# Three slots for the tanh of r, and wider identity products at the start of a gated-recurrence and feed-forward kernel

## The chip, the core and the metric

The kernel runs on one core of one Trainium2 chip. The metric is the device time of an execution in microseconds (us). A profile of one execution lies beside it: its span is the time from the first to the last instruction, and the device time is a few us longer. Engines: PE is TensorE (PEld its weight loads), ACT ScalarE, DVE VectorE, POOL GpSimd, SP the queue that issues the DMAs.

## What is computed

```python
# x, r_gate, i_gate: 4 x 5824 x 256 fp32; a_param: 256
a_base = 1 / (1 + exp(-a_param))
log_a  = 8 * sigmoid(r_gate) * log(clip(a_base))
a_t    = exp(log_a)
norm   = sqrt(maximum(1 - a_t * a_t, 1e-6))
h[t]   = a_t[t] * h[t-1] + norm[t] * sigmoid(i_gate[t]) * x[t]      # scan along the sequence
y      = h.reshape(23296, 256)
out    = (((y @ w1) * (y @ w2)) @ w3) @ w_out                       # 256 -> 1024 -> 256
```

The last two weights are multiplied once at the start (w3 @ w_out, 1024 x 256), so that the main part has three products: y @ w1, y @ w2 and their elementwise product times the folded weight.

## The kernel before

The 23,296 tokens are cut into 47 chunks: two of 256, forty-four of 512, one of 256. A chunk goes through these steps, each a short word in one long string, ORDER, that is read from left to right at the end of the function; the word names the step, the number behind it the chunk. The string is written out by hand or by a planner, and each engine executes its instructions in just that order. Waits come from the tiles: an instruction waits until its inputs are written, and a new tile waits until those who used the slot before have done.

- r, i, x: loads of the three inputs into rings of 4, 5 and 4 slots, issued on SP (line 136).
- R: tanh of r / 2 on ScalarE, with tokens on the partitions, into a bf16 tile th_r (line 145 for the chunks in TURN_R, line 147 for the other 40).
- V: th_r is turned so that channels lie on the partitions. The seven chunks in TURN_R go through TensorE (a product with the identity in transpose mode, line 185, into PSUM), the other 40 through a DMA transpose that SP issues (line 196) into a tile rt.
- d: exp on ScalarE (line 207) gives a_t; s, q: its square and the root of 1 minus it (lines 215, 217, 221).
- I, p, t: tanh of i, plus 1, times x, into a tile u_t; U: u_t is turned as th_r is.
- g, h, y: the gated input, the scan on VectorE (line 249) and the cast to bf16 (line 258).
- a, b: products with w1 and w2 on TensorE (line 268) into PSUM tiles pa and pb; c: pa is copied to SBUF as sa (lines 282, 284); m: sa times pb on VectorE (line 296).
- D: product with the folded weight (line 307); e, o: copied out of PSUM and stored.
- Lw, Cw, Ft, Fc, Fm, Fe: loads, casts and the folding of the weights, all in the first 50 us or so.
- W0 to W15: sixteen heaps of products of the identity with itself, on TensorE (line 263). Nobody reads what they write. They stand in the first part of ORDER, at places where TensorE waits for its first data. The first is ahead of V1; six stand in a row ahead of the turns of U0; two between these turns and those of U1, four behind them, ahead of the first product with w1; three single ones follow later.

A helper, `ring(pool, shape, dtype, name, tag)`, gives the tiles: RINGS holds the number of slots of each tag, and a new tile takes the next slot in turn. th_r has two. So the tanh of a chunk waits for the turn of the chunk whose tanh was two before it in ORDER. The heaps take a tile of tag pb, which has two slots of two PSUM banks each, and which the products with w2 share.

Of the kernel before, what the change touches and what calls it, by code (L numbers as in the profile page):

```python
# [22 lines left out]
def kernel(  # L23
# [12 lines left out]
    nc = tc.nc  # L36
    P = 128
# [11 lines left out]
    CT = 512  # L49
# [16 lines left out]
    ident = consts.tile([P, P], BF16, tag="ident")  # L66
# [31 lines left out]
    STAGE = {'w1': ['a', 'a'], 'w2': ['nrm', 'nrm'], 'wo': ['a', 'nrm'], 'w3': ['a', 'nrm', 'a', 'nrm', 'a', 'nrm',  # L98
        'a', 'nrm']}
    CASTING = set()  # L100
    WARM = [8, 8, 8, 8, 8, 8, 8, 8, 8, 8, 8, 8, 8, 8, 8, 8]
    RINGS = {"r": 4, "i": 5, "x": 4, "th_r": 2, "u": 2, "rt": 2, "ut": 6, "a": 6, "nrm": 6, "h": 2, "y": 4,
             "sa": 3, "g": 3, "ot": 3, "w3": 4, "w3t": 2, "po": 4, "pb": 2}
    taken = dict.fromkeys(RINGS, 0)

    def ring(pool, shape, dtype, name, tag):
        slot = taken[tag] % RINGS[tag]
        taken[tag] += 1
        return pool.tile(shape, dtype, name=name, tag=f"{tag}_{slot}")
# [150 lines left out]
    def warm(i):  # L260
        pp = ring(psum_b, [P, 2, CT], F32, name="warm", tag="pb")
        for _ in range(WARM[i]):
            nc.tensor.matmul(out=pp[:, 0, :P], lhsT=ident, rhs=ident, start=True, stop=True)  # L263

    def up(c, m, dst, w_sb):
        w = sizes[c]
# [150 lines left out]
    def last(c):  # L417
# [15 lines left out]
        "Cwo.": partial(cast_w, "wo"), "Cw3.": partial(cast_w, "w3"),  # L433
        "Ft": fold_t, "Fc": fold_c, "Fm": fold_m, "Fe": fold_e,
        "W": warm, "E": cast_ident, "A3.": rates_turn, "A0.": rates_abs, "A1.": rates_exp, "A2.": rates,
    }

# [171 lines left out]
```

## Time and profile before

| what | value |
|---|---|
| time, median of 3 runs | 517.56 us (516.88 to 517.66) |
| span of the profiled execution | 513.8 us |
| TensorE clock granted | 1.000 |
| identity products | 128, 10.2 us busy, between 2.3 and 21.3 us |
| tanh of r, line 147 | 40, 1065 ns in the mean |
| tanh of r, line 145 | 7, the last at 85.6 us |
| DMA turns of th_r, from issue to landing | 2.4 / 4.4 / 7.1 us (min / median / max) |

In the lines of the profile below, a group is read as line, engine, operation, the tile written and those read, and the shape; "busy" is the union of its instructions' times. Chains of waits and timelines give start and length in us, and "x8" means eight instructions merged into one row. Waits give the total time, the number of times and the longest. A row of one line's own view gives the shortest, the median and the longest duration in ns.

### The profile page before, as it was taken

Reading aid. Unit: us, or ns where it says so; the run is one execution under the profiler, and the core shown is the slowest. Engines: PE = TensorE matmul, PEld = TensorE weight load, DVE = VectorE, ACT = ScalarE, POOL = GpSimd, SP = SyncE. Lnnn points to the kernel's source line nnn. Section 1 sums busy time; section 2 is a strip of 40 time slices with the busy share of each in tenths; the row PEclk is TensorE's granted clock in tenths of the full one; section 3 lists DMA queues with packets and bytes.
Section 4 is the critical chain, followed back from the end, with each engine's and each line's share of the span. In section 5 each row is a group of like instructions: output and inputs, shape, how many; then the busy total and the mean of one; then the engine's idle time right before and its main releaser. Section 6 shows DMA issues by size and latency. Waiting matters only on the chain.

```text
span 513.8 us, 9036 instructions
## 1 busy us (share of the span) xinstructions
PE 499.8 (97%) x3267; PEld 314.2 (61%) x3321; DVE 430.6 (84%) x414; ACT 465.5 (91%) x720; POOL 312.9 (61%) x271
## 2 busy tenths in 40 slices
PE   7889999999999999999999999999999999999997
PEld 7658565566565566556656556564566655656566
DVE  5889999999999889978878799888878697959762
ACT  8899999999999999999999999998998979888543
POOL 2583858646637956866595983957646569480200
PEclk9999999999999999999999999999999999999999
DMA  8997999999989998896999996989795995252112
GB/s 299 410 414 255 305 315 285 312 240 316 314 242 269 266 276 261 221 276 201 289 288 310 262 272 191 234 228 246 197 265 132 215 316 170 101 150 76 54 60 103
DMA packets 177281, 123.82 MB, mean 241 GB/s; under 512 B 86354, under 2 KB 172884, under 8 KB 177236
## 3 DMA queue, kind: packets, MB, share of 16 engines
q1 hardware_dynamic: 177232, 123.23, 84.6%
q8 instruction: 26, 0.43, 0.3%
q14 instruction: 19, 0.16, 0.1%
q10 hardware_dynamic: 4, 0.00, 0.0%
HBM read 78.91 MB, written 23.86 MB: 200 GB/s over the span
## 4 chain that ended last, share of the span: by engine, by line
PE 86%; ACT 5%; DMA 4%; issue 2%; DVE 2%; SPq 1%; ACTq 0%; DVEq 0%
PE po L307 29%; PE pb L268 28%; PE pa L268 27%; DMA r_t<-in_r_gate_dram 4%; ACT sa L284 2%; PE pw L378 1%; PE ptr L185 1%; DVE g_t L296 1%; PE ptw L367 1%; ACT ot L284 1%; SPq L136 1%; DVE h_t L249 1%; ACT i_t L154 1%; ACT a_t L207 1%; ACT L154 0%
## 5 line engine op out<-in xcount | busy, mean ns | idle before, releaser
L296 DVE TENSOR_TENSOR g_t<-sa,pb 128x1024 bf16<-128x1024 bf16 (+1 forms) x188 | 219.0, 1181 | 62.0 <-PE pb L268 29.1
L268 PEld LDWEIGHTS <-w_sb 128*128 128x128 bf16 x1504 | 146.3, 98 | 146.8 <-issue 5.5
L284 ACT CAST sa<-pa 128x512 bf16<-128x512 f32 (+1 forms) x339 | 182.4, 588 | 27.6 <-PE pa L268 18.3
L268 PE MATMUL pa<-y_t,w_sb 128*128 128x512 bf16 (+1 forms) x721 | 185.9, 372 | 4.5 <-ACT sa L284 3.5
L268 PE MATMUL pb<-y_t,w_sb 128*128 128x512 bf16 (+1 forms) x729 | 182.5, 372 | 1.5
L307 PE MATMUL po<-wp_sb,g_t 128*128 128x256 bf16 x1456 | 177.7, 273 | 0.4
L307 PEld LDWEIGHTS <-g_t 128*128 128x128 bf16 x1456 | 142.4, 98 | 40.5 <-issue 0.9
L258 POOL CAST y_t<-h_t 128x1024 bf16<-128x1024 f32 (+1 forms) x46 | 51.2, 1112 | 141.2 <-DVE h_t L249 138.8
L178 POOL TENSOR_TENSOR u_t<-i_t,x_t 128x512 bf16<-128x512 f32 (+1 forms) x89 | 120.0, 1365 | 5.5 <-DMA ut<-u_t 2.5
L249 DVE TENSOR_TENSOR_SCAN h_t<-a_t,h_t,nrm 128x512 f32<-128x512 f32 (+1 forms) x92 | 121.0, 1345 | 1.9
L217 POOL TENSOR_TENSOR nrm<-a_t 128x512 f32<-128x512 f32 (+1 forms) x74 | 81.3, 1116 | 12.8 <-ACT a_t L207 9.9
L207 ACT ACTIVATE a_t<-rt,la 128x512 f32<-128x512 bf16 (+1 forms) x80 | 64.2, 821 | 0.0
L159 POOL TENSOR_SCALAR i_t<-i_t 128x1024 f32<-128x1024 f32 (+1 forms) x45 | 53.4, 1189 | 17.6 <-ACT i_t L154 17.6
L284 ACT COPY ot<-po 128x512 f32<-128x512 f32 (+1 forms) x85 | 49.6, 590 | 11.8 <-PE po L307 11.5
L232 DVE SCALAR_TENSOR_TENSOR nrm<-nrm,ut 128x1024 f32<-128x1024 f32 (+1 forms) x39 | 54.4, 1394 | 5.2 <-ACT nrm L221 5.2
L154 ACT ACTIVATE i_t<-i_t 128x1024 f32<-128x1024 f32 (+1 forms) x47 | 49.2, 1049 | 0.1
L221 ACT ACTIVATE nrm<-nrm 128x1024 f32<-128x1024 f32 (+1 forms) x47 | 48.4, 1040 | 0.2
L147 ACT ACTIVATE th_r<-r_t 128x1024 bf16<-128x1024 f32 (+1 forms) x40 | 42.6, 1065 | 0.0
L282 DVE CAST sa<-pa 128x512 bf16<-128x512 f32 (+1 forms) x37 | 21.9, 617 | 1.4 <-PE pa L268 1.1
L221 ACT ACT_TABLE_LOAD x17 | 21.8, 1283 | 0.4
L215 ACT ACTIVATE nrm<-a_t 128x512 f32<-128x512 f32 (+1 forms) x17 | 10.7, 648 | 0.1
L263 PE MATMUL warm<-ident 128*128 128x128 bf16 x128 | 10.2, 247 | 0.0
(57 smaller groups left out, 132.6 us busy)
## 6 DMA issues: line engine op xcount, KB each, us to landing
out_dram<-ot SPq DMA_DIRECT2D x90, 256.0 KB, 3.4
r_t<-in_r_gate_dram SPq DMA_DIRECT2D x44, 512.0 KB, 5.3
i_t<-in_i_gate_dram SPq DMA_DIRECT2D x44, 512.0 KB, 5.9
x_t<-in_x_dram SPq DMA_DIRECT2D x44, 512.0 KB, 5.9
wf<-in_moe_w_dram SPq DMA_DIRECT2D x12, 512.0 KB, 10.1
wf<-in_moe_w_out_dram SPq DMA_DIRECT2D x2, 512.0 KB, 10.5
r_t<-in_r_gate_dram SPq DMA_DIRECT2D x3, 256.0 KB, 2.7
i_t<-in_i_gate_dram SPq DMA_DIRECT2D x3, 256.0 KB, 3.8
```

The lines of the kernel that those rows point to most:

```text
L154: nc.scalar.activation(out=t[:, :n, :], in_=t[:, :n, :], func=AF.Tanh, scale=0.5)
L159: (nc.vector if c in DV_PLUS else nc.gpsimd).tensor_scalar(t, t, 1.0, 1.0, op0=ALU.add, op1=ALU.mult)
L178: (nc.vector if (c, half) in DV_HALF else nc.gpsimd).tensor_mul(out=u, in0=t, in1=xt)
L207: nc.scalar.activation(out=a, in_=pr, func=AF.Exp, scale=la4[:, cb:cb + 1], bias=la4[:, cb:cb + 1])
L217: (nc.vector if (c, cb) in DV_SQUARE else nc.gpsimd).tensor_mul(out=n, in0=a, in1=a)
L221: nc.scalar.activation(out=T["n", c][:, :, :w], in_=T["n", c][:, :, :w], func=AF.Sqrt, scale=-1.0, bias=1.0)
L232: nc.vector.scalar_tensor_tensor(out=T["n", c][:, :, :w], in0=T["n", c][:, :, :w], scalar=1e-3, in1=T["pu", c][:, :, :w], op0=ALU.max, op1 ...
L249: nc.vector.tensor_tensor_scan(h[:, cb, :], a[:, cb, :], n[:, cb, :], init, ALU.mult, ALU.add)
L268: nc.tensor.matmul(out=dst[:, :w], lhsT=w_sb[:, cb, m * P:(m + 1) * P], rhs=T["y", c][:, cb, :w], start=(cb == 0), stop=(cb == NCB - 1))
L284: nc.scalar.copy(out=dst, in_=src_ps)
L296: nc.vector.tensor_mul(out=T["g", c][:, 2 * mp:2 * mp + 2, :w], in0=T["sa", c, mp][:, :, :w], in1=T["pb", c, mp][:, :, :w])
L307: nc.tensor.matmul(out=po, lhsT=T["g", c][:, k, j * P:(j + 1) * P], rhs=wp_sb[:, k, :], start=(k == 0), stop=(k == KD - 1), skip_group_che ...
```

## The change

Two tables and one instruction are changed. The ring of th_r gets a third slot: the tanh of a chunk now waits for the turn of the one three before it. SBUF tiles that are placed behind it move up by one slot, 2 KB a partition. Each of the sixteen heaps of identity products has two matmuls instead of eight. Each of them has the identity, repeated four times along the columns, as its moving operand, and writes 512 columns, a whole PSUM bank, where it wrote 128. ORDER is unchanged.

```diff
-    WARM = [8, 8, 8, 8, 8, 8, 8, 8, 8, 8, 8, 8, 8, 8, 8, 8]
-    RINGS = {"r": 4, "i": 5, "x": 4, "th_r": 2, "u": 2, "rt": 2, "ut": 6, "a": 6, "nrm": 6, "h": 2, "y": 4,
+    WARM = [2] * 16
+    RINGS = {"r": 4, "i": 5, "x": 4, "th_r": 3, "u": 2, "rt": 2, "ut": 6, "a": 6, "nrm": 6, "h": 2, "y": 4,
              "sa": 3, "g": 3, "ot": 3, "w3": 4, "w3t": 2, "po": 4, "pb": 2}
...
     def warm(i):
         pp = ring(psum_b, [P, 2, CT], F32, name="warm", tag="pb")
         for _ in range(WARM[i]):
-            nc.tensor.matmul(out=pp[:, 0, :P], lhsT=ident, rhs=ident, start=True, stop=True)
+            nc.tensor.matmul(out=pp[:, 0, :].rearrange("p (n q) -> p n q", q=P), lhsT=ident,
+                             rhs=ident.unsqueeze(1).broadcast_to([P, CT // P, P]), start=True, stop=True)
```

## The prediction

> **What bounds the kernel now.** I read the page first, then the chain of waits cut to its first 36 us, then ScalarE's waits, then the rows of the two tanh lines, and last the timeline of TensorE.
>
> The page's head and its chain:
>
> ```profile
> span 513.8 us, 9036 instructions
> ...
> PE 499.8 (97%) x3267; PEld 314.2 (61%) x3321; DVE 430.6 (84%) x414; ACT 465.5 (91%) x720; POOL 312.9 (61%) x271
> ...
> PE 86%; ACT 5%; DMA 4%; issue 2%; DVE 2%; SPq 1%; ACTq 0%; DVEq 0%
> ```
>
> TensorE is busy 97% of the span and carries 86% of the chain. Cut into stretches, busy time against length is 99.42 of 100 us between 200 and 300, 99.19 between 300 and 400, 99.42 between 400 and 500. Summed over 30 to 500 us TensorE is idle for 3.10 us. So from about 30 us on the time is the sum of the matmuls, and neither edit touches one of those.
>
> The start is different. This is the chain before 36 us (start, length, what):
>
> ```profile
> 5.24 8.59 DMA r_t<-in_r_gate_dram
> ...
> 13.91 10.40 DMA r_t<-in_r_gate_dram
> ...
> 24.37 1.28 ACT L145
> 25.67 1.06 ACT th_r L145
> 26.72 0.67 ACT a_t L207
> 27.39 0.27 ACT sa L284
> ...
> 27.70 0.38 PE pa L268 x2
> ```
>
> Two loads of r stand behind each other from 5.24 to 24.30 us, while the DMA engines run at 1.04 to 1.06 busy and 406 to 413 GB/s (10 to 25 us). ScalarE waits for the second one (r4), then TensorE waits for ScalarE. All the identity heaps lie before 21.3 us, in the shadow of this.
>
> **What the Trainium skill says.** "TensorE: Matmul & The Clock Gate", Part 1: start to start a matmul costs N/1.2 GHz while the clock is cold (106.7 ns for 128 columns, 426.7 for 512) and N/2.4 GHz plus about 2.5 ns when warm (55.6 and 215.7). The clock is lifted after a busy window of some 3.4 us whose phase is free; it counts time, not instructions. The trace agrees. The heap row below has 48 products in 4.38 us; less one latency (219 ns, the median of the row) that is 4.16 us for 47 steps, 88.5 ns each. With 107 and 56 ns that makes 30 cold ones, 3.2 us, so the lift is at about 8.7 us. Counted by half microseconds, the products are 7 or 8 up to 8.5 us and 13 from 9.0 on. "PSUM — Partial Sum Buffer", the four PSUM rules: one matmul writes at most one bank, 512 fp32 columns; the new product fills just that. "SBUF — State Buffer", Who interferes with whom: TensorE reads through its own ports and waits for no other engine. No run here tests that alone.
>
> **The identity products.** Sixteen heaps of 8 matmuls over 128 columns become sixteen heaps of 2 over 512: the same 1024 columns. The heaps in the timeline of TensorE:
>
> ```profile
> 2.31 1.03 PE L263 MATMUL warm<-ident 128*128 128x128 bf16 x8
> ...
> 5.48 4.38 PE L263 MATMUL warm<-ident 128*128 128x128 bf16 x48
> 9.70 0.39 PE L185 MATMUL ptr<-ident,u_t 128*128 128x128 bf16 x4
> 9.92 1.06 PE L263 MATMUL warm<-ident 128*128 128x128 bf16 x16
> 10.82 0.39 PE L185 MATMUL ptr<-ident,u_t 128*128 128x128 bf16 x4
> 11.04 1.95 PE L263 MATMUL warm<-ident 128*128 128x128 bf16 x32
> 12.97 1.03 PE L268 MATMUL pa<-y_t,w_sb 128*128 128x256 bf16 x8
> ```
>
> First heap: 8 x 107 = 856 ns becomes 2 x 427 = 854. In the run of six, the cold 3.2 us stays, and the 18 warm products, 18 x 56 = 1008 ns, become 4.5 x 216 = 972. The 72 products after 9.9 us (16, 32 and three heaps of 8) go from 72 x 56 = 4.03 us to 18 x 216 = 3.89. Together 0.18 us less of TensorE. The weight loads go from 128 to 32, 96 x 98 ns = 9.4 us of PEld, but they run beside the products (56 ns a step is the product's own rate), so nothing more. Since TensorE's array sees the same columns at the same rate, I expect the lift at the same place.
>
> What of the 0.18 us reaches the end? The heaps hold back the turns of u (ptr) and the first pa. The first four turns end at 9.70 + 0.39 = 10.09, and VectorE's product that reads them starts at 10.29 because of ScalarE's root, whose first of two ends about 9.63 + 1.15 / 2 = 10.21. So an earlier end of the heaps gives nothing there. The first pa (12.97) follows the cast of y_t, 12.30 + 0.61 = 12.91, and not the heap, which ended at 12.77 + its latency. The last two heaps (19.64, 20.66) are followed by 2.19 us of TensorE waiting for ScalarE at 27.70. The cover is the r4 load; were it gone, the most is the whole 0.18. I take 0, bounds -0.18 and, if a moving operand that repeats its 128 columns four times were read at half the rate (no row here has such an operand; the nearest, pa and po, read plain runs), twice the duration of the 24 matmuls ahead of the first pa: 24 x 216 ns = 5.2 us, less the slack worked out under the slower rival, so +3.9. Nothing in the trace or the pages gives a reason for that, so it gets the far edge only.
>
> The tile that a heap takes (tag pb) and its place in the ring don't change, so the waits before it and the next pb tile's stay.
>
> **The third slot.** ScalarE's tanh of r in chunk c wrote the slot of the tanh two before, so it waited for that chunk's turn: 7 chunks are turned by TensorE, 40 by DMA. With three slots it waits for the turn three before. ScalarE's waits (us in total, times, longest), and then two rows of line 147's own view (min/median/max ns, first and last start):
>
> ```profile
> ACT sa L284 <- PE pa L268: 18.3, 28, 2.5
> ACT ot L284 <- PE po L307: 11.5, 12, 3.3
> ACT sa L284 <- DVE g_t L296: 8.2, 9, 1.6
> ACT th_r L145 <- DMA r_t<-in_r_gate_dram: 1.6, 2, 0.9
> ```
>
> ```profile
> L147 ACT ACTIVATE th_r<-r_t x40: 645/1070/1143, 46.6 to 449.1; 128x1024 bf16<-128x1024 f32 x39, 128x512 bf16<-128x512 f32 x1
> L147 ACTq EVENT_SEMAPHORE  x8: 17/17/17, 48.1 to 338.7; - x8
> ```
>
> In the list of waits no tanh waits for a turn at all: its only waits are for r's own load, 1.6 us and 1.2 for its table load. The page's group of line 147 has 0.0 us of idle before its 40 tanhs. I then laid the start of each tanh beside the issue of the DMA turn two tanhs before: the closest pair is chunk 12's tanh at 85.64 with chunk 11's turn issued at 80.53, 5.11 us; the next is 6.48, all others 7.0 or more. The turn's landing takes 4.4 us at the median, 7.1 at most. So the wait was always over. The single one that might have bound, r4's tanh, needed chunk 3's turn by TensorE, whose products start at 23.30 and end at 23.91, before its load at 24.30. Gain of the slot: 0. Bounds: the 0.1 us idle before line 147's table loads, and the eight semaphore instructions there, 8 x 17 ns = 0.14, if they vanish. Nothing waits more, because the instruction order on each queue is unchanged and the added wait is older than the removed one.
>
> What else moves: the tiles behind th_r in SBUF lie 2 KB further on. 2,048 is a multiple of the 16-byte lines that the SBUF page names, so I cost it at 0.
>
> **The sum.** 513.8 - 0 to 0.3 = 513.5 to 513.8 of span. The median of the runs, 517.56, lies 3.76 above the span; so 517.5.
>
> **Rivals.** *Faster*: my reading of the waits is too coarse, and the looser slot lets a stretch like 178 to 197 us, where the chain leaves TensorE for ScalarE and VectorE, close up. For it: ScalarE is 91% busy. Against it: ScalarE works in a fixed order and no tanh waits. Price: TensorE's idle between 30 and 500 us is 3.10 us in all; half of it gone gives 516.0. *Slower*: the clock. If two long products a heap do not lift it as eight short ones do, all heaps run cold. Six heaps then last 12 x 427 = 5.12 us, 0.98 more; the 16 and the 32 products 0.85 and 1.71 more; eight turns 8 x 51 = 0.4. The first pa comes 3.9 us late. It decides from the point where the slack is used up: 0.12 us at the root (10.09 against 10.21) and the 1.18 us that ScalarE idles before r4 at 24.37, 1.3 together. What is over, 2.6 us, shifts all of TensorE's later work: 520.2. (All of this is an estimate from the rows above and the cold price.) Against it: the array is busy for the same time. *Scatter*: with three runs 0.78 us apart, the same work may land anywhere in 516.5 to 518.6.
>
> **How the numbers follow.** A difference within 0.2% (1.0 us) is about what a measurement of this kernel cannot tell from none. No change 0.68, faster 0.14, slower 0.18 (the cold clock 0.10, something in the 2 KB shift or the repeated operand 0.08). The likeliest case has 516.5 to 518.6; the range reaches to the faster rival's 516.0 and some way to 520.2, so 516.0 to 519.4.
>
> **What would show it.** After: 32 products in heaps of 2, about 216 ns apart when warm; the six heaps together still ending near 9.6 us; the first pa near 12.97; r4's tanh still starting with its load near 24.3; line 147 with 0.0 idle; TensorE's idle from 30 to 500 us near 3 us. I am wrong if the first pa is more than 1.3 us late, if a tanh's start moves ahead of its place on ScalarE, or if the idle in that stretch changes by over 1 us.

## The result: 0.31% faster, and the gain hangs on one table load

The changed kernel took 515.42 us (median of 11 runs, 514.12 to 516.12). The kernel before took 516.80 us (median of 11, 515.16 to 518.14; the three runs of the prediction are among these, at the upper side). The ratio of the medians is 0.9969, with a 95% interval of 0.9955 to 0.9983: 0.9 to 2.3 us gained. The time lies below the 516.0 to 519.4 us that were forecast.

The page of the changed kernel, its head and its chain:

```profile
span 512.4 us, 8840 instructions
...
PE 500.2 (98%) x3171; PEld 308.7 (60%) x3225; DVE 428.0 (84%) x414; ACT 465.6 (91%) x720; POOL 312.8 (61%) x271
...
PE 90%; ACT 4%; DMA 3%; issue 1%; SPq 1%; DVE 1%; ACTq 0%; DVEq 0%
```

The span is 1.4 us shorter. TensorE's own busy time hardly changed (499.8 to 500.2 us). Its share of the chain rose from 86% to 90%, some 20 us, but that is not the gain: the chain of the kernel before leaves TensorE for ScalarE and VectorE from 177.98 to 197.13 us, that of the changed kernel does not, and TensorE is busy for 5.95 of the 6.00 us from 182 to 188 in both. In the kernels below that gain nothing the share is 90%, too.

The two timelines of ScalarE around chunk 4's tanh, first of the kernel before, then of the changed one (start and length in us, then idle time ahead of it and what ended that):

```profile
22.14 1.06 ACT L221 ACTIVATE nrm<-nrm 128x1024 f32<-128x1024 f32 x1
24.37 1.28 ACT L145 ACT_TABLE_LOAD   x1 [1.18 <-DMA r_t<-in_r_gate_dram]
25.67 1.06 ACT L145 ACTIVATE th_r<-r_t 128x1024 bf16<-128x1024 f32 x1
```

```profile
22.10 1.06 ACT L221 ACTIVATE nrm<-nrm 128x1024 f32<-128x1024 f32 x1
23.17 1.28 ACT L145 ACT_TABLE_LOAD   x1
24.47 1.06 ACT L145 ACTIVATE th_r<-r_t 128x1024 bf16<-128x1024 f32 x1
```

Before, ScalarE had nothing to do from 23.2 us on, waited until r4 had landed, and only then loaded the tanh table. After, the same load begins at once and is over about when r4 is there. The tanh starts 1.20 us earlier. What held the table load is shown by the row of line 145's semaphore instructions (instructions by which a program waits for a signal): the kernel before has two, the first at 24.3 us, and the changed kernel has none. This is the row of the kernel before:

```profile
L145 ACTq EVENT_SEMAPHORE  x2: 17/17/17, 24.3 to 82.8; - x2
```

The compiled programs say the same. These are ScalarE's instructions for the tanh of chunk 4 in order, with what each waits for (DMAHW2 is the signal that r4's load gives, PE TensorE's; LoadActFuncSet is the table load):

```
before   EventSemaphore [waits DMAHW2]   LoadActFuncSet   Activation th_r [waits PE]
after                                    LoadActFuncSet   Activation th_r [waits DMAHW2]
```

With two slots the tanh of chunk 4 had two things to wait for: its load, and TensorE's turn of chunk 3, which still read the slot. One of the waits stayed with the tanh. The other, the DMA, went ahead of the table load that stands before the tanh, as a semaphore instruction of 17 ns. With three slots the second wait is gone from this instruction, so the remaining one is carried by the tanh itself, behind the table load.

In these two profiles the gain goes on to TensorE. Rows of its timeline, first of the kernel before, then of the changed one:

```profile
14.96 0.62 PE L185 MATMUL ptr<-ident,th_r 128*128 128x128 bf16 x8 [0.96 <-ACT th_r L145]
...
27.70 0.38 PE L268 MATMUL pa<-y_t,w_sb 128*128 128x256 bf16 x2 [2.19 <-ACT sa L284]
...
35.17 1.04 PE L378 MATMUL pw<-wo_sb,w3t 128*128 128x256 bf16 x8
...
507.07 3.66 PE L307 MATMUL po<-wp_sb,g_t 128*128 128x256 bf16 x32
```

```profile
5.68 5.33 PE L263 MATMUL warm<-ident 128*128 128x512 bf16 x12
...
14.01 1.03 PE L269 MATMUL pa<-y_t,w_sb 128*128 128x256 bf16 x8
14.95 0.61 PE L185 MATMUL ptr<-ident,th_r 128*128 128x128 bf16 x8
...
26.50 0.38 PE L269 MATMUL pa<-y_t,w_sb 128*128 128x256 bf16 x2 [1.24 <-ACT sa L285]
...
34.18 1.04 PE L379 MATMUL pw<-wo_sb,w3t 128*128 128x256 bf16 x8
...
505.66 3.66 PE L308 MATMUL po<-wp_sb,g_t 128*128 128x256 bf16 x32
```

The pause ahead of pa is 1.24 us where it was 2.19, and it ends at 26.50, not at 27.70. The product pw (a part of the folding of the weights) starts at 34.18 us, where it was 35.17: 0.99 us ahead. The rest of the 1.4 us, 0.42, lies between pw and the last 32 products (471.90 us before, 471.48 after). A table among the experiments shows that this part is not the change's, and that single profiles of one kernel differ by as much as the whole gain. The identity products were no help: six heaps took 5.33 us instead of 4.38, and the first pa was 1.04 us late. It cost nothing: TensorE's pause of 0.96 us ahead of the next turn took it up, and that turn starts at 14.95 instead of 14.96.

### The profile page after: what moved, and what is told of

The parts are those of the page before. It is cut to its first block, busy times and chain, and to the rows that moved or that the text cites. A ratio compares the mean times of both kernels' runs of the same rounds, so it can differ in the third digit from the quotient of the medians.

```text
span 512.4 us, 8840 instructions
## 1 busy us (share of the span) xinstructions
PE 500.2 (98%) x3171; PEld 308.7 (60%) x3225; DVE 428.0 (84%) x414; ACT 465.6 (91%) x720; POOL 312.8 (61%) x271
## 4 chain that ended last, share of the span: by engine, by line
PE 90%; ACT 4%; DMA 3%; issue 1%; SPq 1%; DVE 1%; ACTq 0%; DVEq 0%
PE po L308 30%; PE pb L269 29%; PE pa L269 28%; DMA r_t<-in_r_gate_dram 2%; DMA i_t<-in_i_gate_dram 1%; PE pw L379 1%; ACT sa L285 1%; PE ptr L185 1%; SPq L136 1%; PE ptw L368 1%; DVE h_t L249 0%; ACT th_r L145 0%; ACT a_t L207 0%; ACT ot L285 0%; ACT L154 0%
## 5 line engine op out<-in xcount | busy, mean ns | idle before, releaser
L249 DVE TENSOR_TENSOR_SCAN h_t<-a_t,h_t,nrm 128x512 f32<-128x512 f32 (+1 forms) x92 | 119.7, 1331 | 1.9
L221 ACT ACT_TABLE_LOAD x17 | 21.8, 1283 | 0.3
L263 PE MATMUL warm<-ident 128*128 128x512 bf16 x32 | 11.1, 490 | 0.0
```

The costliest lines, as they stand in the source:

```text
L221: nc.scalar.activation(out=T["n", c][:, :, :w], in_=T["n", c][:, :, :w], func=AF.Sqrt, scale=-1.0, bias=1.0)
L249: nc.vector.tensor_tensor_scan(h[:, cb, :], a[:, cb, :], n[:, cb, :], init, ALU.mult, ALU.add)
```

## Experiments

Theories: the *split wait* (above: one of the tanh's two waits stands ahead of its table load), the *heaps* (fewer and longer identity products), and the *main part* (looser slots close later stalls, the faster rival of the prediction). Each ratio is to the kernel before, run beside it, with its 95% interval in brackets.

### Each part alone

```diff
-    RINGS = {... "th_r": 2, ...
+    RINGS = {... "th_r": 3, ...
```

> Third slot alone, heaps of eight as before. Split-wait theory (the tanh of chunk 4 had two waits; one of them was carried by a semaphore instruction ahead of its table load, so the load of the tanh table could not begin before r4 had landed): table load near 23.2 us and tanh near 24.5 instead of 24.37 and 25.67, TensorE resumes near 26.5 instead of 27.7, time 1.0 to 1.6 us shorter, ratio 0.997 to 0.998. Heap theory (the gain is from fewer, longer identity products): same as before, ratio 0.9995 to 1.0005. Main-part theory (looser slots close later stalls): a gain that appears only after 40 us, nothing before.

Measured: 0.9978 (0.9967 to 0.9989). ScalarE in this kernel:

```profile
23.30 1.28 ACT L145 ACT_TABLE_LOAD   x1
24.60 1.06 ACT L145 ACTIVATE th_r<-r_t 128x1024 bf16<-128x1024 f32 x1
```

Then the identity products alone: two of 512 columns a heap, th_r with two slots.

> Wide identity products alone, two slots as before. Split-wait theory: chunk 4's tanh stays near 25.67, ratio 0.9995 to 1.001. Heap theory: the whole gain, ratio 0.996 to 0.998. Main-part theory: ratio about 1.000.

Measured: 0.9998 (0.9986 to 1.0010). ScalarE:

```profile
23.93 1.28 ACT L145 ACT_TABLE_LOAD   x1 [0.98 <-DMA r_t<-in_r_gate_dram]
25.22 1.06 ACT L145 ACTIVATE th_r<-r_t 128x1024 bf16<-128x1024 f32 x1
```

The slots bring the gain, and the table load moves with them, as the split wait had it. The wide products alone change nothing that can be measured, and the wait ahead of the table load stays, 0.98 us. In this execution r4 landed near 23.9 instead of 24.3, so the tanh, too, is 0.45 us earlier than before: the landing is not the same in every execution, and what counts is the 1.29 us from the start of the table load to the tanh.

### Is it the table load?

The next kernel keeps two slots and eight products, and loads the table early by other means: a tanh of 128x2 numbers that nobody reads afterwards, step Z, just ahead of chunk 4's tanh. In the diff, the changed line of ORDER is shown whole.

```diff
+    def early_tanh():
+        nc.scalar.activation(out=zt, in_=zt, func=AF.Tanh)
...
     steps = {
+        "Z": early_tanh,
...
-        U2 a1.3.1 s2.1 Cwo.1 i3 Fc2 V3 x3 Lw3.0 q2 Lw3.1 i4 Lw3.4 m1.1 c1.3.0 Fm2 R4 g2 h2.0 h2.1 d3.0 Lw3.7 c1.3.1
+        U2 a1.3.1 s2.1 Cwo.1 i3 Fc2 V3 x3 Lw3.0 q2 Lw3.1 i4 Lw3.4 m1.1 c1.3.0 Fm2 Z R4 g2 h2.0 h2.1 d3.0 Lw3.7 c1.3.1
```

> The kernel before with one tanh of 128x2 numbers (unused afterwards) put on ScalarE just ahead of chunk 4's tanh, so that the table is loaded while r4 is still under way; slots and heaps as before. Split-wait theory: table load near 23.2, chunk 4's tanh near 24.7, time 0.8 to 1.2 us shorter, ratio about 0.998. Heap and main-part theories: one more instruction and nothing gained, ratio 1.000 to 1.0005.

Measured: 0.9976 (0.9965 to 0.9987). ScalarE:

```profile
23.38 1.28 ACT L421 ACT_TABLE_LOAD   x1
24.68 0.20 ACT L421 ACTIVATE zt<-zt 128x2 f32<-128x2 f32 x1
24.87 1.06 ACT L145 ACTIVATE th_r<-r_t 128x1024 bf16<-128x1024 f32 x1
```

One useless tanh of 0.20 us on 128x2 numbers gives as much as the third slot. The wait is still there, but now behind the table load.

The next kernel keeps the whole change and gives back the second wait to chunk 4's tanh alone, by putting it into the slot of chunk 3's.

```diff
-        t = ring(gates, [P, NCB, 4, P], BF16, name="th_r", tag="th_r")
+        slot = {4: 2, 7: 1}.get(c, taken["th_r"] % 3)
+        taken["th_r"] += 1
+        t = gates.tile([P, NCB, 4, P], BF16, name="th_r", tag=f"th_r_{slot}")
```

> The changed kernel, but chunk 4's tanh takes the slot that chunk 3's tanh had, and chunk 7's takes the one left over; all other tanhs keep three slots. Split-wait theory: chunk 4's tanh has two waits again, its table load starts at 24.3 to 24.4 and it at about 25.7; the 1.0 to 1.2 us are lost, ratio 0.9985 to 1.000. Heap and main-part theories: the gain stays, ratio about 0.997.

Measured: 1.0008 (0.9996 to 1.0020). ScalarE:

```profile
24.30 1.28 ACT L147 ACT_TABLE_LOAD   x1 [1.22 <-DMA r_t<-in_r_gate_dram]
25.60 1.06 ACT L147 ACTIVATE th_r<-r_t 128x1024 bf16<-128x1024 f32 x1
```

With the second wait back at one of 47 tanhs the whole gain is gone (the ratio lies even a little above the forecast's 0.9985 to 1.000), though the slots of all the others but chunk 7's, the wide products and the 2 KB shift are as in the changed kernel. This settles what the gain hangs on, and it leaves nothing measurable to the other parts.

How the gain gets from there into the time is another question. Each execution's record has the mean clock granted to TensorE. The kernel before and these four ran side by side; these are their numbers of executions with the median time of each (us), and the length of TensorE's pause ahead of pa in the profile (us):

| kernel | clock 0.999 or 1.000 | clock 0.993 to 0.997 | pause |
|---|---|---|---|
| before | 29, 515.55 | 46, 517.17 | 2.19 |
| wide products alone | 10, 515.45 | 12, 517.07 | 2.27 |
| chunk 4 in the old slot | 6, 515.54 | 16, 517.47 | 2.26 |
| three slots alone | 22, 515.05 | none | 1.30 |
| early table | 22, 515.17 | none | 0.89 |

A clock of 0.997 over 515 us loses 1.5 us of full clock, about the 1.62 us between the two groups of the kernel before. Where the table load is held, 74 of 119 executions have the lower clock; where it is not, none of 44. At full clock, three slots gain 0.50 us and the early table 0.38 (95% intervals by resampling 0.2 to 0.8 and -0.1 to 0.8), of 1.74 and 1.62 between the medians of all executions. So most of the gain here is that executions with the lower clock no longer occur. All profiles are of executions at 0.999 or 1.000, so where in the span the clock is lower is not seen; that the longer pause of TensorE lets it fall fits the last column, but is not shown. On the chip of the last two experiments the kernel before has 516.85 at full clock (6 executions) and 516.61 at 0.997 (5), and the changed kernel gains 1.34 us at full clock (515.51, 5 executions). How the gain divides stays open.

For the main part, these are numbers from TensorE's timelines (start of the pw product, start of the last 32 products, and the difference, us). The repeat of the changed kernel is described further below.

| kernel | pw | last products | between |
|---|---|---|---|
| before | 35.17 | 507.07 | 471.90 |
| changed | 34.18 | 505.66 | 471.48 |
| three slots alone | 34.25 | 505.74 | 471.49 |
| wide products alone | 34.72 | 506.20 | 471.48 |
| early table | 34.93 | 506.63 | 471.70 |
| chunk 4 in the old slot | 35.10 | 506.58 | 471.48 |
| changed, repeated | 35.53 | 507.08 | 471.55 |

The kernel with two slots and wide products has the same 471.48 us as the changed one. So the 0.42 us of the first comparison are not due to the slots; two kernels with two slots and narrow products took 0.2 and 0.4 us more, one with three slots and narrow products did not. I take it for scatter of single executions. That it was scatter is not shown. The first column scatters more: the repeat of the changed kernel reached pw at 35.53, later than the kernel before, though its median was 515.51. So the 0.99 us at pw is a reading of one pair of profiles, not the size of the gain.

### The heaps

No identity products, all else as changed (`WARM = [0] * 16`):

> The changed kernel with no identity products at all. My slack of the prediction holds if chunk 4's tanh still starts near 24.5. Then the clock is lifted later, by real work alone; if by 25 us, ratio to before 0.997 to 0.999; if TensorE stays cold into the dense part after 28 us, up to 3 us at half speed, ratio 1.000 to 1.003. If the heaps are idle filling: 0.997.

Measured: 0.9986 (0.9976 to 0.9996), a median of 516.18. The matmuls show the clock:

```profile
13.34 1.86 PE L269 MATMUL pa<-y_t,w_sb 128*128 128x256 bf16 x8 [3.47 <-POOL y_t L258]
...
17.56 0.95 PE L269 MATMUL pb<-y_t,w_sb 128*128 128x256 bf16 x4
18.34 0.60 PE L269 MATMUL pa<-y_t,w_sb 128*128 128x256 bf16 x4
```

Eight matmuls take 1.86 us where they took 1.03; from 18.3 us on four take 0.60, as in the changed kernel. Chunk 4's tanh starts at 24.86. So the clock comes up some 7 us later than in the changed kernel (18.3 us against the end of the six heaps at 11.0). The medians of the two are 0.8 us apart (516.18 against 515.42), but they did not run side by side and their intervals overlap: what the heaps bring is not shown. All 19 executions have a mean granted clock of 0.999 or 1.000 on record, the profiled one, cold until 18.3 us, too: this mean does not count the cold stretch at the start. At that clock the kernel before took 516.10 beside them (10 executions).

Twice as many wide products (`WARM = [4] * 16`):

> The changed kernel with four wide products a heap instead of two, thirteen of the sixteen heaps ahead of the first pa. The first pa comes 4 to 5 us later, near 17.5. By the slack of the prediction (1.3 us) TensorE's dense part begins about 3 us later, ratio to before about 1.003; if the shadow of the r4 load is wider than that, ratio 0.997 to 1.000.

Measured: 1.0052 (1.0033 to 1.0070), a median of 519.74:

```profile
5.99 7.71 PE L263 MATMUL warm<-ident 128*128 128x512 bf16 x24
...
19.16 1.04 PE L269 MATMUL pa<-y_t,w_sb 128*128 128x256 bf16 x8
20.06 0.61 PE L185 MATMUL ptr<-ident,th_r 128*128 128x128 bf16 x8
```

The first pa is 6.2 us later than before the change (12.97), and chunk 4's tanh came at 29.53, 5.06 us later than in the changed kernel. So 1.1 us of slack was taken up, near the 1.3 us that the prediction worked out; but that is luck, for it is not the same slack. Of the 1.3, 1.18 were ScalarE's idle time ahead of r4's table load, and the change had already used those. What took up the 1.1 is TensorE's pause ahead of the turn behind the first pa, 0.96 us in the kernel before, which the prediction did not count: that turn, at 20.06, is only 5.10 us later. My forecasts of the first pa (near 17.5) and of the ratio (about 1.003) were both too low.

### A version that goes further?

Chunk 4's tanh stands ahead of the two exps of chunk 3, which don't need r4. Moved behind them (cut out of two lines of ORDER, joined here):

```diff
-... R4 g2 h2.0 h2.1 d3.0 Lw3.7 c1.3.1 m0.2 d3.1 Lw3.5 ...
+... g2 h2.0 h2.1 d3.0 Lw3.7 c1.3.1 m0.2 d3.1 R4 Lw3.5 ...
```

> The changed kernel with chunk 4's tanh moved behind both exps of chunk 3 on ScalarE, so that they no longer stand behind r4's load. Split-wait theory: the first exp needs a table load, and this one now carries a DMA wait of its own; if that DMA has landed, the exps run near 24.5 instead of 25.4 and TensorE resumes near 25.6 instead of 26.5, but pa of chunk 2 still needs y2 near 28.3, so at most 0.3 us more than the changed kernel, ratio to before 0.996 to 0.998. If it has not, the table load waits for it and part of the gain is lost, ratio 0.998 to 1.001. If r4's load alone set the pace, another whole 1 us, ratio 0.995.

Measured: 0.9957 (0.9942 to 0.9973). The same with the small tanh ahead of the exps, `Z g2 h2.0 h2.1 d3.0`:

> The same with one tanh of 128x2 numbers (unused afterwards) ahead of chunk 3's exps, which loads the table with no wait before it. Split-wait theory: exps near 24.7 whatever the DMA does, ratio to before 0.996 to 0.998, not slower than the changed kernel by more than 0.05%. If r4's load alone set the pace: 0.995.

Measured: 0.9948 (0.9928 to 0.9969). Both came out below the forecast of 0.996 to 0.998, at the 0.995 of the rival that r4's load alone sets the pace. So the change and this last kernel ran once more, side by side:

> The changed kernel once more, beside the next one on one chip. Ratio to before 0.996 to 0.998, as it was; the six heaps in a row end at another place than 11.0 us, since their length (5.33 us in the first profile, 4.28 to 4.32 in the later kernels with wide products) followed the clock and not the width.

Measured: 0.9967 (0.9955 to 0.9979).

> The changed kernel with chunk 3's exps ahead of chunk 4's tanh and one small tanh ahead of them, once more. If it is a real gain over the change: ratio to before 0.994 to 0.996, below the changed kernel's by 0.001 to 0.002; if the first reading was scatter, the same as the changed kernel.

Measured: 0.9962 (0.9948 to 0.9977). The two differ by 0.0005, far inside their intervals. A gain over the change is not shown. The new stop is visible in TensorE's timeline of the first profile of this kernel:

```profile
27.34 0.61 PE L185 MATMUL ptr<-ident,th_r 128*128 128x128 bf16 x8 [0.46 <-ACT wp_sb L414]
28.56 0.60 PE L269 MATMUL pb<-y_t,w_sb 128*128 128x256 bf16 x4 [0.62 <-DVE g_t L297]
```

TensorE resumes earlier (25.62) and then stops for ScalarE and VectorE before the 512-column products begin at 29.10 (28.35 in the changed kernel).

The repeat of the change is of use for the heaps and for r4. Its timelines of TensorE and ScalarE:

```profile
5.75 4.60 PE L263 MATMUL warm<-ident 128*128 128x512 bf16 x12
```

```profile
23.53 1.28 ACT L145 ACT_TABLE_LOAD   x1
25.14 1.06 ACT L145 ACTIVATE th_r<-r_t 128x1024 bf16<-128x1024 f32 x1 [0.33 <-DMA r_t<-in_r_gate_dram]
```

Six heaps of wide products took 5.33 us once, 4.60 here, and 4.28 to 4.84 in five other profiles; narrow ones 4.06, 4.38 and 4.79. They overlap: the width is not what made the first 5.33. And here r4 landed at about 25.1, after the table load. Then the tanh follows it at once, whereas in the kernel before a table load of 1.28 us would still have come between.

## Why the prediction was wrong

- *The third slot, "Gain of the slot: 0".* This is the step that failed, and within it the bound: "the eight semaphore instructions there, 8 x 17 ns = 0.14, if they vanish". I counted them by their own length, and only those of line 147. The one that mattered was on line 145. Its length is 17 ns; what it did was to hold everything behind it, a table load of 1.28 us, until r4 had landed. In the pair of profiles its removal brought 1.20 us at the tanh and 0.99 at pw; in the medians, three slots alone brought 1.74 us, of which 0.50 show at full clock. The rest goes with the executions at the lower clock, and the prediction has no term for those.
- *"The wait was always over."* That was right: chunk 3's turn had ended at 23.91, before r4's 24.30. No waiting time for the slot was removed. What was removed is the presence of a second wait, which decided on which side of the table load the other one stood. The sign was on the lines shown: the chain had the table load at 24.37, behind the landing, although a table load needs no r. I did not ask why it came so late.
- *The Trainium skill* bears on this in "ScalarE: Activation LUTs", What ACT_TABLE_LOAD costs (1283 ns a load), and under its step-by-step stages: the compiler places the load right before the instruction that needs it. The trace agrees on both, 1283 ns each time and in that place. Of a wait ahead of the load the two places say nothing; the runs show it. The page adds a drain of some 1380 ns, 2.66 us in all for a change of tables; here the tanh starts 1.30 us after the load's start, and no row stands between them, so the measured cost is 1.30.
- *The identity products.* Cost 0 was right: 0.9998 alone. That the six heaps would end near 9.6 us was wrong (about 11.0), but the delay of 1.04 us was covered. It was not covered by the slack worked out under the slower rival (0.12 us at the root and 1.18 ahead of r4) but by TensorE's own pause of 0.96 us at 14 us. The repeated operand is not read at half the rate: a warm wide product steps at 216 ns as a plain one (four in 1.03 us, of which the last takes 0.379: three steps of 217).
- *What bounds the kernel.* The dense part from 30 us on was right, and its idle time stayed near 3 us. But the idle time that I summed for the faster rival began at 30 us, just behind TensorE's pause of 2.19 us. That rival had the sign right and, as far as the profiles show, the place wrong.
- *The level.* "3.76 above the span" was not overhead. In the changed kernel's profiled run the device time, 514.32, is 1.9 above the span of 512.4. By this the profile of the kernel before is of an execution of about 515.7 us (an estimate: 513.8 and 1.9), shorter than all three runs given, and these lay 0.76 us above the median of eleven. Of the 2.1 us by which the forecast missed, this is about a third; the other 1.38 us is what the change gained.

## What to carry to other kernels

A wait that is over early is not free if the instruction has another one: ask which of its waits are carried by the instruction and which ahead of it, and what stands between. Where a table load appears in a chain behind a DMA, it can be moved into the DMA's time by leaving the activation a single wait, or by a tiny activation of the same table just before it. Price a semaphore instruction by what it holds back, not by its own length. Before a difference of medians is put down to a difference of two timelines, compare executions of equal clock: with three slots alone the gain was 1.74 us over all executions and 0.50 at full clock.

## What was not expected of the hardware

A table load in this trace takes 1283 ns, and the activation behind it, where it waits for nothing else, starts 1.29 to 1.30 us after the load has begun; nothing else was seen between the two. The same six heaps of identity products took 5.33 us in one execution of the changed kernel and 4.60 in another: how long the cold stretch lasts is not a property of the program alone. Nor is the clock granted afterwards: of 75 executions of the kernel before on one chip, 29 had a mean of 1.000 and 46 one of 0.996 or 0.997, 1.62 us apart in the median.
